# VectorE's queue order around a state's sums: where the product of k and b with R and the transpose of the inverse are issued

## The chip, the core and the metric

The kernel runs on one core of a Trainium2 chip. TensorE (PE) multiplies matrices into PSUM; VectorE (DVE), ScalarE (ACT) and GpSimd (POOL) work elementwise; SyncE (SP) issues most DMA transfers. Each engine takes the instructions of its own queue in order. The metric is the time of one execution on the device in microseconds; the median of several executions is compared.

## The reference

Three stages, all in float32. A recurrence over 768 steps for 32 pairs of batch and head, each with a state of 40 x 40; an MLP with squared ReLU over the 3072 tokens; and a layer of 8 experts that each token passes through by its largest logit.

```
for t in range(S):
    y[:, :, t] = einsum('bhd,bhde->bhe', rt, state)
    Sa = einsum('bhde,bhe->bhd', state, at)
    state = state * wt[:, :, None, :] - einsum('bhd,bhe->bhde', Sa, bt) + einsum('bhd,bhe->bhde', vt, kt)
...
h = x @ w_in; r = maximum(h, 0); x = (r * r) @ w_out
...
out[i] = gate_w[i] * (maximum(disp[e] @ w1[e], 0) @ w2[e])[pos[i]]
```

## The kernel before

The recurrence is turned into products of matrices. The 768 steps are cut into NS = 12 segments of 64 steps, each of NC = 2 chunks of 32. Within a chunk the steps depend on each other through a triangular system of 32 x 32 per head, so each segment needs the inverses of such matrices; the state goes from chunk to chunk. All segments run in a Python loop that is unrolled, over s and in it over c.

For a segment s these pieces matter:

- `scale(s)` (L133 to L160) loads w and then k and b (L138, L140), forms running products R of the decays w by a scan (L115), and multiplies k and b by them in place, two instructions (L146). A second scan (L128) gives their inverses, which scale a. It is a generator: its pieces are put between other work, for segment s + 2 during segment s, and the two instructions of L146 are traced after the first two slots of chunk (s, 1). The scan of L128 uses the one buffer that R has, so it follows L146.
- `lower(s, c)` (L162) multiplies a by k and b on PE and forms the triangular matrices; `invert(s)` (L183) transposes them on DVE (L187, tile `solve_al`) and then inverts them on GpSimd by 31 steps of two instructions each (recorded at L280, tiles `tmp` and `solve_tl`). `inverted(s)` (L203) transposes the result on DVE (L207, tile `solve_tf`), and ACT (L210) and DVE (L211) pick from it what is needed (tile `tt`).
- Chunk (s, c) goes through slots a to g (L1399 to L1450): `out` of the chunk before (PE product `py`, DVE L379 makes y), `right` (`pr`, reads the state zv and a), `solve` (`psa`, reads `tt`), `turn`, `inner`, `mix` (`ppq`, DVE L369 makes `lr`), `other` of the chunk before and `step`. The last two call `update` (L285): 16 products on PE per half of the heads into `pn`, and then two sums on DVE (L296) that write the next state, zk for `other` and zv for `step`. At a segment's end `other` also scales zk by a decay (L389).
- `fetch` (L248) loads the inputs of the next chunk and multiplies zk by `rx`, on DVE (L273) or on GpSimd.

In chunk (s, 0) `lower` and `invert` for segment s + 1 are traced, at the end of chunk (s, 1) `inverted(s + 1)`, behind both calls of `step`. Into the slots, pieces of the MLP of earlier tokens are put (`bursts`, L668): products `pl` on PE (L434), ReLU on ACT (L632), square on DVE (L634, tile `g`), a split into a high part on ACT (`gh`, L396) and a difference on DVE (`gl`, L397), and products that accumulate (`acc`, L616).

The order on each engine: PE's instructions keep the order of the program (`keep_in_program_order`), and GpSimd's of the recurrence are chained one behind another (`pool`, L277, with `issue_after`). For DVE, ACT and the DMA queues a scheduler orders the instructions ahead of time: it simulates the engines and issues, of what is ready in its simulation, what was traced first (or was given a higher priority). The hardware then follows this order. An instruction whose input comes later on the chip than in the simulation holds up its queue.

`tc.issue_after(i)` adds an edge from instruction i to each instruction of i's engine that is traced in its block: issue order alone, without a semaphore.

Of the kernel before, what the change touches and what calls it, by code (L numbers as in the profile page):

```python
# [16 lines left out]
ALU = mybir.AluOpType  # L17
# [13 lines left out]
C = 32  # L31
NC = SC // C
SEG = SC + 1
# [4 lines left out]
ROWS = 64 + D  # L38
# [19 lines left out]
BY_COL = [slice((1 - j) * 64, (1 - j) * 64 + D) for j in range(2)]  # L58
# [3 lines left out]
class Rwkv:  # L62
# [6 lines left out]
    def __init__(self, ctx, tc, ps, consts, keep, wd, kb, ad, rv, wl, tok, rng):  # L69
        self.tc, self.nc, self.ps = tc, tc.nc, ps  # L70
        self.c = consts
        self.src = dict(wd=wd, kb=kb, ad=ad, rv=rv, wl=wl, tok=tok)
        nc = self.nc
        p1 = ctx.enter_context(tc.tile_pool(name="rw1", bufs=1))
        self.p = ctx.enter_context(tc.tile_pool(name="rwr", bufs=1))
        self.dram = ctx.enter_context(tc.tile_pool(name="rwdram", bufs=2, space=DRAM))
        self.sq = p1.tile([128, 16, SEG], F32, name="seed_q")
        self.w = keep.tile([128, 1 + 16 * SEG], F32, tag="w_d", name="w_d")
        self.kb = keep.tile([128, 2, 16, SC], F32, tag="kb_d", name="kb_d")
        self.gb = p1.tile([128, 16, D], F32, name="g_b")  # L80


        self.a = [p1.tile([128, NC, 2, 16, C], F32, name=f"a{i}") for i in range(2)]
        self.zv = [p1.tile([128, 2, 16, D], F32, name=f"zv{i}") for i in range(2)]
        self.lr = [p1.tile([128, 2, 16, C], F32, name=f"lr{i}") for i in range(2)]
        self.zk = [p1.tile([128, 2, 16, D], F32, name=f"zk{i}") for i in range(2)]
        self.rng = rng

        nc.gpsimd.memset(self.w[32:64], 0.0)
        nc.vector.memset(self.kb[32:64], 0.0)  # L90
        nc.gpsimd.memset(self.a[0][32:64, :, 1], 0.0)
        nc.vector.memset(self.sq, 0.0)
        for t in (self.a[1][32:64, :, 1], *(t[32:64, 1] for t in self.zv + self.lr + self.zk), self.gb[32:64]):
            nc.gpsimd.memset(t, 0.0)
        for t in (self.zv[0], self.zk[0]):
            nc.gpsimd.memset(t[0:64, 1], 0.0)
            nc.gpsimd.memset(t[64:128, 0], 0.0)
        self.last = None
        self.pre, self.rt = {}, {}

    def psum(self, name):
# [31 lines left out]
    def scale(self, s):  # L133

        nc, src = self.nc, self.src
        w, kb, a = self.w, self.kb, self.a[s % 2]
        for j in range(2):
            nc.sync.dma_start(out=w[BY_COL[j]], in_=src["wd"][s, j])  # L138
        for j in range(2):
            nc.sync.dma_start(out=kb[BY_COL[j]], in_=src["kb"][s, j])  # L140

        pr = self.products(w, 16, ROWS, s)
        r = next(pr)
        yield
        for k in range(2):
            nc.vector.tensor_mul(kb[:ROWS, k], kb[:ROWS, k], r[:ROWS, :, 1:SEG])  # L146
            yield
        g = self.tile([128, 16], f"g64.{s}", 2)
        nc.vector.tensor_copy(g[:ROWS], r[:ROWS, :, 0])
        self.pre[s] = [g, [None] * NC, None]  # L150
        for j in range(2):
            nc.sync.dma_start(out=a[BY_COL[j], :, j].rearrange("p c n t -> p c (n t)"), in_=src["ad"][s, j])
        q = next(pr)
        yield
        for j in range(2):
            v = a[BY_COL[j], :, j]
            self.times(s == 0 and j == 0, out=v, in0=v, in1=q[BY_COL[j], :, 0:SC].rearrange("p n (c t) -> p c n t", c=NC))
        self.wl = self.tile([128, 1 + 10 * SEG], f"wl.{s}", 1)
        nc.sync.dma_start(out=self.wl, in_=src["wl"][s])
        yield  # L160
# [42 lines left out]
    def inverted(self, s):  # L203

        nc, tl = self.nc, self.tl
        tf = self.tile([128, C, 2, NC, H], f"solve.tf{s}", 2)
        nc.vector.transpose(out=tf.rearrange("p t u c h -> p (t u c h)"),  # L207
                            in_=tl[:, :, :, None].to_broadcast([128, C, C // 2, 2]))
        tt = self.tile([128, C, NC, H], f"tt.{s}", 2)
        nc.scalar.mul(tt, tf[:, :, 0], self.c["odd"][:, 0:1])  # L210
        i = nc.vector.scalar_tensor_tensor(out=tt, in0=tf[:, :, 1], scalar=self.c["odd"][:, 1:2], in1=tt,  # L211
                                           op0=ALU.mult, op1=ALU.add)
        self.pre[s][2] = tt
        return i.ins
# [33 lines left out]
    def fetch(self, s, c):  # L248
# [17 lines left out]
        for j in range(2):  # L266
            v = zk[BY_STEP[j], j].rearrange("p (h y) e -> p y h e", y=2)
            self.times(c == 1, out=v, in0=v, in1=rx[BY_STEP[j]])

    def times(self, fast, **k):  # L270

        if fast:
            self.nc.vector.tensor_tensor(op=ALU.mult, **k)  # L273
        else:
            self.pool(self.nc.gpsimd.tensor_tensor, op=ALU.mult, **k)
# [9 lines left out]
    def update(self, s, c, z, l, r, half):  # L285

        nc = self.nc
        pn = self.psum(f"pn{s}_{c}_{half}")[:, 0:8 * D].rearrange("p (n e) -> p n e", n=8)
        for n in range(8):
            i = half * 8 + n  # L290
            for j in range(2):
                rows = BY_STEP[j]
                self.mm(pn[BY_COL[j], n], lhsT=l[rows, j, i], rhs=r[rows, j, i], start=True, stop=True)
        for j in range(2):
            rows, ns = BY_COL[j], slice(half * 8, half * 8 + 8)
            nc.vector.tensor_tensor(out=z[c ^ 1][rows, j, ns], in0=z[c][rows, j, ns], in1=pn[rows], op=ALU.add)  # L296

    def right(self, s, c):

# [26 lines left out]

    def step(self, s, c, half):

        self.update(s, c, self.zv, self.zk[c], self.zv[c], half)

    def decay(self, s):

# [49 lines left out]

    def other(self, s, c, half):

        self.update(s, c, self.zk, self.zv[c], self.zk[c], half)
        if half == 1 and c == NC - 1 and s + 1 < NS:
            for j in range(2):
                v = self.zk[c ^ 1][BY_COL[j], j]
                self.nc.vector.tensor_mul(v, v, self.gb[BY_COL[j]])  # L389

# [1197 lines left out]
```

## Time and profile before

| | |
|---|---|
| median of 3 runs | 1195.83 us (1195.64 to 1196.54) |
| profiled execution | 1200.53 us, its span 1198.7 us |
| mean granted clock of PE | 0.927 of full |
| PE, DVE busy | 969.2 us (81%), 915.0 us (76%) |
| ACT, POOL busy | 491.7 us (41%), 570.5 us (48%) |
| segments of the recurrence in their steady state | about 187 to 821 us |
| experts | from about 880 us |

The busy shares are means over stages with different limits, so they don't tell what bounds a stage; the rows below are from the recurrence. A line such as L280 or L397 can be a helper's: L280 is all of GpSimd's recurrence, and L397 all differences of a split. PEld is the loading of weights into PE. "Idle before" is the time that an engine stood still ahead of an instruction, with what ended it. In the timelines neighbouring instructions of one kind are merged (x2, x4).

### The profile page before, as it was taken

What the parts mean: (1) busy time and instruction counts of PE and PEld (TensorE: products, weight loads), DVE (VectorE), ACT (ScalarE), POOL (GpSimd) and SP (SyncE); (2) the same over time, 40 slices, a digit from 0 to 9 for tenths busy, and PEclk for the clock granted to TensorE, in tenths of its full rate; (3) what the DMA queues carried; (4) which work ended last, traced back from release to release, by engine and by line L of the source; (5) the groups of instructions that cost most, each with busy time, mean ns of one, the idle gap of its engine ahead of it and who ended that gap; (6) DMA issues with size and microseconds to landing.
All of it is one profiled execution on the core that took longest, in us unless ns stands there. A gap on an engine that the chain in (4) does not pass through costs nothing.

```text
span 1198.7 us, 42394 instructions
## 1 busy us (share of the span) xinstructions
PE 969.2 (81%) x17749; PEld 901.3 (75%) x17749; DVE 915.0 (76%) x1925; ACT 491.7 (41%) x1301; POOL 570.5 (48%) x912
## 2 busy tenths in 40 slices
PE   1665446688989898979899797998989998999993
PEld 1554346677878787878788787887979998999993
DVE  8999887586878878686868788675867886777770
ACT  2443222233424232423324232342337475767760
POOL 5773936548283856648282847554000032222220
PEclk9999978898888888989989898999999999999997
DMA  8724524653343534343433535233267275767630
GB/s 243 201 80 132 153 57 108 232 141 116 102 122 102 132 104 125 107 132 107 131 116 86 132 104 141 87 118 92 86 193 245 77 238 183 218 198 223 219 95 8
DMA packets 87610, 164.37 MB, mean 137 GB/s; under 512 B 16313, under 2 KB 46651, under 8 KB 86444
## 3 DMA queue, kind: packets, MB, share of 16 engines
q1 hardware_dynamic: 78476, 141.47, 40.8%
q10 hardware_dynamic: 6048, 11.06, 3.2%
q0 software_dynamic: 2880, 8.98, 2.2%
q8 instruction: 143, 2.34, 0.8%
q14 instruction: 63, 0.52, 0.1%
HBM read 137.23 MB, written 16.29 MB: 128 GB/s over the span
## 4 chain that ended last, share of the span: by engine, by line
PE 29%; POOL 25%; DVE 20%; DMA 11%; issue 9%; ACT 4%; SPq 1%; POOLq 0%; ACTq 0%; DVEq 0%
POOL solve_tl L280 13%; POOL tmp L280 12%; PE upl L434 6%; PE uacc L1114 6%; PE acc L616 6%; PE pl L434 4%; DMA out_dram<-uo,room 2%; DVE zv L296 2%; DMA xg<-x_dram,room 2%; DVE gl L397 2%; DMA kb_d<-in_kb_dram 2%; DMA stage_hi<-in_w_out_dram 2%; DVE g L634 2%; DVE rq_r L115 1%; DVE solve_tf L207 1%
## 5 line engine op out<-in xcount | busy, mean ns | idle before, releaser
L280 POOL TENSOR_TENSOR solve_tl<-solve_tl,tmp 128x126 f32<-128x126 f32 (+22 forms) x372 | 195.0, 524 | 29.1
L280 POOL TENSOR_TENSOR tmp<-solve_al,solve_tl 128x126 f32<-128x126 f32 (+22 forms) x372 | 186.4, 501 | 33.1 <-DVE a L180 4.9
L616 PE MATMUL acc<-woh,gh 128*128 128x328 f32 x384 | 133.6, 348 | 12.9 <-ACT gh L396 12.7
L616 PE MATMUL acc<-woh,gl 128*128 128x328 f32 x384 | 130.1, 339 | 9.1 <-DVE gl L397 8.8
L616 PE MATMUL acc<-wol,gh 128*128 128x328 f32 x384 | 126.5, 329 | 0.0
L434 PE MATMUL pl<-x_hi,wi_hi 128*128 128x256 f32 x384 | 121.8, 317 | 1.7 <-ACT x_hi L446 1.7
L434 PE MATMUL pl<-x_lo,wi_hi 128*128 128x256 f32 x384 | 113.4, 295 | 11.0 <-DVE x_lo L449 11.0
L434 PE MATMUL pl<-x_hi,wi_lo 128*128 128x256 f32 x384 | 113.0, 294 | 0.0
L280 POOL MEMSET solve_tl<- 128x512 f32 x12 | 6.3, 527 | 215.4 <-DVE solve_al L187 215.4
L396 ACT CAST gh<-g 128x512 fp32r<-128x512 f32 x96 | 59.5, 620 | 120.2 <-DVE g L634 112.8
L1192 POOL DMA_INDIRECT out_dram<-uo,room x30 | 34.1, 1136 | 155.2 <-DVE uo L1181 84.1
L1122 POOL DMA_INDIRECT xg<-x_dram,room x30 | 30.4, 1012 | 141.6 <-DVE gl L397 61.4
L632 ACT ACTIVATE g<-pl 128x512 f32<-128x512 f32 x96 | 57.6, 600 | 97.2 <-PE pl L434 96.8
L397 DVE TENSOR_TENSOR gl<-g,gh 128x512 fp32r<-128x512 f32 x96 | 71.9, 749 | 26.4 <-ACT gh L396 26.3
L616 PEld LDWEIGHTS acc<-woh,gh 128*128 128x128 f32 x384 | 77.9, 203 | 17.0 <-ACT gh L396 13.3
L616 PEld LDWEIGHTS acc<-woh,gl 128*128 128x128 f32 x384 | 78.0, 203 | 15.3 <-DVE gl L397 14.6
L1114 PE MATMUL uacc<-w2h,hh 128*128 128x320 f32 x240 | 77.0, 321 | 12.0 <-ACT wi_hi L1070 12.0
L434 PEld LDWEIGHTS pl<-x_lo,wi_hi 128*128 128x128 f32 x384 | 78.1, 203 | 11.3 <-DVE x_lo L449 11.3
L283 PE MATMUL pr<-zv,a 104*32 104x40 f32 (+1 forms) x1536 | 44.0, 245 | 50.2 <-DVE zv L296 32.1
L434 PEld LDWEIGHTS pl<-x_hi,wi_hi 128*128 128x128 f32 x384 | 77.6, 202 | 6.5 <-ACT x_hi L446 2.1
L283 PEld LDWEIGHTS pr<-zv,a 104*32 104x32 f32 (+1 forms) x1536 | 31.7, 143 | 62.2 <-DVE zv L296 42.5
L616 PEld LDWEIGHTS acc<-wol,gh 128*128 128x128 f32 x384 | 78.2, 204 | 0.0
(272 smaller groups left out, 3030.6 us busy)
## 6 DMA issues: line engine op xcount, KB each, us to landing
wol<-wol SPq DMA_DIRECT2D x96, 328.0 KB
w<-in_w_dram SPq DMA_DIRECT2D x30, 640.0 KB
w<-in_w_dram SPq DMA_DIRECT2D x30, 512.0 KB
kb_d<-in_kb_dram SPq DMA_DIRECT2D x24, 320.0 KB
zv<-in_tok_dram SPq DMA_DIRECT2D x48, 160.0 KB
zk<-in_tok_dram SPq DMA_DIRECT2D x48, 160.0 KB
rx<-rt SPq DMA_DIRECT2D x192, 40.0 KB
w<-in_w_dram SPq DMA_DIRECT2D x30, 256.0 KB
```

Of the source, the lines that this page charges most:

```text
L280: self.last = f(*a, **k).ins
L283: self.tc.keep_in_program_order(self.nc.tensor.matmul(*a, **k))
L296: nc.vector.tensor_tensor(out=z[c ^ 1][rows, j, ns], in0=z[c][rows, j, ns], in1=pn[rows], op=ALU.add)
L396: return (nc.scalar.copy(hi, x).ins, nc.vector.tensor_tensor(out=lo, in0=x, in1=hi.bitcast(F32), op=ALU.subtract).ins)
L397: nc.vector.tensor_tensor(out=lo, in0=x, in1=hi.bitcast(F32), op=ALU.subtract).ins)
L434: tc.keep_in_program_order(tc.nc.tensor.matmul(out, lhsT=a, rhs=b, start=n == 0, stop=n == len(seq) - 1))
L616: self.tc.keep_in_program_order(self.nc.tensor.matmul(*a, **k))
L632: nc.scalar.activation(g, pl, AF.Relu)
L634: nc.vector.tensor_tensor(out=g, in0=pl, in1=g, op=ALU.mult)
L1114: self.tc.keep_in_program_order(self.nc.tensor.matmul(*a, **k))
L1122: nc.gpsimd.indirect_dma_start(out=xg[:, 0:DX], out_offset=None, in_=self.x1, in_offset=bass.IndirectOffsetOnAxis(ap=self.idx[2 * j + t], ...
L1192: self.nc.gpsimd.indirect_dma_start(out=self.out, out_offset=bass.IndirectOffsetOnAxis(ap=self.to[:, n:n + 1], axis=0), in_=o[:, t], in_of ...
```

## The change

`step` and `other` now remember the last of their instructions on DVE, in `sums[0]` (last sum of zv) and `sums[1]` (last sum of zk, or its scaling by the decay). A new function `behind(n)` opens `issue_after` for the first n of them. The two products of k and b with R (L146) are traced behind both, the transpose of the inverse (L207) behind the last sum of zv. Nothing else changes: no instruction is added, removed or altered. For segments 0 and 1 of `scale` and segment 0 of `inverted` no sums have been traced yet, so they have no edges; that leaves ten pairs of products and eleven transposes with one.

```diff
--- before.py
+++ after.py
@@ -96,6 +96,7 @@
             nc.gpsimd.memset(t[0:64, 1], 0.0)
             nc.gpsimd.memset(t[64:128, 0], 0.0)
         self.last = None
+        self.sums = []
         self.pre, self.rt = {}, {}
 
     def psum(self, name):
@@ -143,7 +144,8 @@
         r = next(pr)
         yield
         for k in range(2):
-            nc.vector.tensor_mul(kb[:ROWS, k], kb[:ROWS, k], r[:ROWS, :, 1:SEG])
+            with self.behind(2):
+                nc.vector.tensor_mul(kb[:ROWS, k], kb[:ROWS, k], r[:ROWS, :, 1:SEG])
             yield
         g = self.tile([128, 16], f"g64.{s}", 2)
         nc.vector.tensor_copy(g[:ROWS], r[:ROWS, :, 0])
@@ -204,8 +206,9 @@
 
         nc, tl = self.nc, self.tl
         tf = self.tile([128, C, 2, NC, H], f"solve.tf{s}", 2)
-        nc.vector.transpose(out=tf.rearrange("p t u c h -> p (t u c h)"),
-                            in_=tl[:, :, :, None].to_broadcast([128, C, C // 2, 2]))
+        with self.behind(1):
+            nc.vector.transpose(out=tf.rearrange("p t u c h -> p (t u c h)"),
+                                in_=tl[:, :, :, None].to_broadcast([128, C, C // 2, 2]))
         tt = self.tile([128, C, NC, H], f"tt.{s}", 2)
         nc.scalar.mul(tt, tf[:, :, 0], self.c["odd"][:, 0:1])
         i = nc.vector.scalar_tensor_tensor(out=tt, in0=tf[:, :, 1], scalar=self.c["odd"][:, 1:2], in1=tt,
@@ -267,6 +270,13 @@
             v = zk[BY_STEP[j], j].rearrange("p (h y) e -> p y h e", y=2)
             self.times(c == 1, out=v, in0=v, in1=rx[BY_STEP[j]])
 
+    def behind(self, n):
+
+        order = ExitStack()
+        for i in self.sums[:n]:
+            order.enter_context(self.tc.issue_after(i))
+        return order
+
     def times(self, fast, **k):
 
         if fast:
@@ -293,7 +303,8 @@
                 self.mm(pn[BY_COL[j], n], lhsT=l[rows, j, i], rhs=r[rows, j, i], start=True, stop=True)
         for j in range(2):
             rows, ns = BY_COL[j], slice(half * 8, half * 8 + 8)
-            nc.vector.tensor_tensor(out=z[c ^ 1][rows, j, ns], in0=z[c][rows, j, ns], in1=pn[rows], op=ALU.add)
+            i = nc.vector.tensor_tensor(out=z[c ^ 1][rows, j, ns], in0=z[c][rows, j, ns], in1=pn[rows], op=ALU.add)
+        return i.ins
 
     def right(self, s, c):
 
@@ -326,7 +337,7 @@
 
     def step(self, s, c, half):
 
-        self.update(s, c, self.zv, self.zk[c], self.zv[c], half)
+        self.sums[:1] = [self.update(s, c, self.zv, self.zk[c], self.zv[c], half)]
 
     def decay(self, s):
 
@@ -382,11 +393,12 @@
 
     def other(self, s, c, half):
 
-        self.update(s, c, self.zk, self.zv[c], self.zk[c], half)
+        last = self.update(s, c, self.zk, self.zv[c], self.zk[c], half)
         if half == 1 and c == NC - 1 and s + 1 < NS:
             for j in range(2):
                 v = self.zk[c ^ 1][BY_COL[j], j]
-                self.nc.vector.tensor_mul(v, v, self.gb[BY_COL[j]])
+                last = self.nc.vector.tensor_mul(v, v, self.gb[BY_COL[j]]).ins
+        self.sums[1:] = [last]
```

## Rows read from the trace of the kernel before

**Rows 1.** The page's part 1: busy time of each engine, share of the span, instructions.

```profile
PE 969.2 (81%) x17749; PEld 901.3 (75%) x17749; DVE 915.0 (76%) x1925; ACT 491.7 (41%) x1301; POOL 570.5 (48%) x912
```

**Rows 2.** Windows, a segment each: length, busy PE PEld DVE ACT POOL, clock, DMA.

```profile
390.50:456.70 66.20, 58.24 (x1325) 52.86 (x1324) 52.18 (x88) 22.82 (x52) 40.67 (x69) 0.90 0.42 117
sum 601.50, PE 512.30 PEld 465.85 DVE 464.88 ACT 203.88 POOL 363.70; mean PE 56.92 PEld 51.76 DVE 51.65 ACT 22.65 POOL 40.41
```

**Rows 3.** Chain of waits, 394 to 466 us, shares by line.

```profile
by line: POOL solve_tl L280 23.9%; POOL tmp L280 18.2%; DMA kb_d<-in_kb_dram 10.5%; PE acc L616 10.0%; PE pl L434 8.8%; issue 5.6%; DVE kb_d L146 3.7%; PE pa L283 2.9%; DVE zv L296 2.7%; PE pn L283 2.3%; DVE gl L397 2.2%; PE ppq L283 2.0%; 
```

**Rows 4.** Timeline of GpSimd: start, length, what; in brackets idle before and its releaser.

```profile
456.84 0.53 POOL L280 MEMSET solve_tl<- 128x512 f32 x1 [20.50 <-DVE solve_al L187]
```

**Rows 5.** Windows: from a transpose of the inverse (L207) to the next L187.

```profile
428.01:455.45 27.44, 24.88 (x628) 22.23 (x628) 25.13 (x45) 13.18 (x31) 8.18 (x4) 0.88 0.30 92
```

**Rows 6.** Waits, 187 to 821 us, DVE and PE: total us, times, longest.

```profile
DVE solve_tf L207 <- POOL solve_tl L280: 49.3, 10, 9.9
DVE kb_d L146 <- DMA kb_d<-in_kb_dram: 21.9, 9, 2.9
...
PE py L283 <- DVE zk L389: 44.8, 18, 8.7
```

**Rows 7.** Timeline of DVE at the products of k and b.

```profile
397.17 2.56 DVE L146 TENSOR_TENSOR kb_d<-kb_d,rq_r 104x1024 f32<-104x1024 f32 x2 [2.32 <-DMA kb_d<-in_kb_dram]
399.76 1.78 DVE L389 TENSOR_TENSOR zk<-zk,g_b 40x640 f32<-40x640 f32 x2
...
402.30 1.00 DVE L296 TENSOR_TENSOR zv<-zv,pn 40x320 f32<-40x320 f32 x2
...
404.19 1.00 DVE L296 TENSOR_TENSOR zv<-zv,pn 40x320 f32<-40x320 f32 x2
```

**Rows 8.** Timeline of PE: py, the products for the sums of zv, psa.

```profile
400.76 0.23 PE L283 MATMUL py<-zk,lr 104*32 104x40 f32 x2 [3.26 <-DVE zk L389]
...
424.27 1.42 PE L283 MATMUL pn<-zv,zk 64*40 64x40 f32 x64
...
438.27 1.29 PE L283 MATMUL psa<-rh,tt 32*32 32x40 f32 x64
```

**Rows 9.** Timeline of DVE at the transpose of the inverse.

```profile
428.01 1.25 DVE L207 STREAM_TRANSPOSE solve_tf<-solve_tl 128x1024 f32<-128x1024 f32 x1 [4.14 <-POOL solve_tl L280]
429.18 0.65 DVE L634 TENSOR_TENSOR g<-pl,g 128x512 f32<-128x512 f32 x1
429.86 1.00 DVE L296 TENSOR_TENSOR zv<-zv,pn 40x320 f32<-40x320 f32 x2
430.79 0.88 DVE L211 SCALAR_TENSOR_TENSOR tt<-solve_tf,ct,tt 128x512 f32<-128x512 f32 x1
431.70 1.00 DVE L296 TENSOR_TENSOR zv<-zv,pn 40x320 f32<-40x320 f32 x2
432.62 1.65 DVE L397 TENSOR_TENSOR gl<-g,gh 128x512 fp32r<-128x512 f32 x1
```

**Rows 10.** Timeline of DVE, the second transpose of the inverse.

```profile
154.19 1.25 DVE L207 STREAM_TRANSPOSE solve_tf<-solve_tl 128x1024 f32<-128x1024 f32 x1 [8.22 <-POOL solve_tl L280]
```

**Rows 11.** Timeline: a difference on DVE, and three steps of the inverse on GpSimd.

```profile
394.17 0.68 DVE L397 TENSOR_TENSOR gl<-g,gh 128x512 fp32r<-128x512 f32 x1
...
393.25 0.31 POOL L280 TENSOR_TENSOR solve_tl<-solve_tl,tmp 128x58 f32<-128x58 f32 x1
...
394.00 1.02 POOL L280 TENSOR_TENSOR solve_tl<-solve_tl,tmp 128x56 f32<-128x56 f32 x1
...
403.10 0.38 POOL L280 TENSOR_TENSOR tmp<-solve_al,solve_tl 128x110 f32<-128x110 f32 x1
```

**Rows 12.** Windows: PE ahead of the solve.

```profile
434.33:441.00 6.67, 6.67 (x116) 6.15 (x117) 6.24 (x13) 2.70 (x9) 2.01 (x1) 0.61 0.29 89
```

**Rows 13.** Timeline of DVE and of PE in the segment at 224 us.

```profile
224.24 1.25 DVE L207 STREAM_TRANSPOSE solve_tf<-solve_tl 128x1024 f32<-128x1024 f32 x1 [9.88 <-POOL solve_tl L280]
...
234.20 0.31 PE L283 MATMUL pr<-zv,a 104*32 104x40 f32 x2 [4.07 <-DMA zv<-in_tok_dram]
```

## The prediction

> **What bounds the kernel now.** I read the page first: over the span TensorE (PE) is busy 81%, VectorE (DVE) 76% and GpSimd (POOL) 48% [rows 1]. No engine is full, so the question is which wait ends last where the change acts. That is the recurrence, from about 187 to 821 us: nine segments that repeat every 66.8 us (601.5 / 9), in which PE works 56.9 us and DVE 51.7 us in the mean [rows 2]. Next I read the chain of waits over one segment: GpSimd's two lines of the inverse hold 24% and 18% of it, the longest part; most of the rest is PE work [rows 3]. The reader should see a loop in it. GpSimd inverts for segment s+1; DVE transposes the result (L207); from that the solve of (s+1, 0) starts on PE; after it PE, ACT and DVE come to the transposed input (L187) of the next inverse, and GpSimd starts again. GpSimd itself stood idle 20.5 us before that start [rows 4]. So the period is the time of one inverse and its start plus the stretch from L207 to L187. In the segment shown that stretch is 27.44 us (428.01 to 455.45) [rows 4, 5], and the inverse about 66.2 - 27.4 - 1.2 = 37.5 us.
>
> Then I read who makes DVE wait between 187 and 821 us: the transpose waits for GpSimd in ten segments, 49.3 us together, and the product of k and b waits for its load in nine, 21.9 us [rows 6]. DVE runs its queue in order, so what stands behind these two waits too. The timeline shows what that is. Behind the products of k and b (idle 2.32 us, then 2.56 us of work) stand the scaling of zk and the state's sums at 402.30 and 404.19 [rows 7]; PE, which needs them, idles (3.26 us before py in this place alone [rows 8], 44.8 us over the nine segments for the scaled zk [rows 6]). Behind the transpose, which waited 4.14 us, stand one square of the MLP, the four sums of zv and a difference gl [rows 9], though the products for those sums had ended at 425.69 (424.27 + 1.42) [rows 8].
>
> **The change part by part.** It adds no instruction and takes none away; it adds issue order on one engine, without semaphores. The edges concern ten pairs of products and eleven transposes. In one transpose (154.19) [rows 10] the sums had been issued long before, so ten are left; of the products nine pairs stand ahead of sums now, as [rows 7] shows for one.
>
> *The transpose.* Each of the ten goes behind the last sum of its segment. The wait for GpSimd is not removed: the inverse ends when it ends. What changes is that DVE does useful work in the wait. The four sums (2 x 1.00), the square (0.65) and gl leave the stretch after the transpose. The square and gl carry no edge, but they are traced before the transpose and become ready about with the sums, so I expect the planner to let them pass too; that is a choice, and its failure is a rival. gl took 1.65 us where it stood [rows 9], while GpSimd multiplied beside it, and about 0.68 at 394.17 in an empty surrounding [rows 11]. So 3.33 to 4.30 us leave the stretch; I take 4.30, since that is what these instructions cost there. DVE was busy 25.13 us of the 27.44 us [rows 5], so the stretch is nearly DVE's own length and the removal carries through; of the 2.31 us in which it idled I count half, 1.15 us, as going too, since PE, which DVE waited for in them, comes earlier. The bounds of that are 0 and 2.31.
>
> Against it stands what is added beside the inverse. A step of GpSimd that should last about 0.3 us lasted 1.02 when gl ran beside it; beside the sums, which read PSUM, a step lasted 0.38 [rows 11]. So gl costs the inverse 0.7 us, and the sums nothing. (The Trainium skill, SBUF — State Buffer, Who interferes with whom, says why only gl counts: an instruction of VectorE with two inputs in SBUF blocks a GpSimd instruction that reads SBUF, one with at most one does not. The rows agree; if every sum blocked as well, the gain of a segment would shrink by 2.0 us.)
>
> Per segment: 4.30 + 1.15 - 0.7 = 4.75 us; bounds 3.33 - 0.7 = 2.6 and 4.30 + 2.31 = 6.6.
>
> PE must be able to follow. The inverse's second half was ready when L211 ended (430.79 + 0.88 = 431.67) [rows 9], but the solve's product psa began at 438.27 [rows 8], 6.6 us later, because PE was still waiting for sums and gl and then ran its accumulation at a granted clock of 0.61 [rows 12], mostly the lower level of 1.2 GHz, after idling. With the sums early, that work is done before the transpose. So PE gives up to 6.6 us, and DVE is the tighter of the two.
>
> *The products of k and b.* They move behind the scaling of zk and four sums. Their load, which ended at about 397.2, is then there before they are reached: DVE saves the 2.32 us of idling, and the sums come 2.32 + 2.56 = 4.9 us earlier. For whom? The queue behind the products (the scan of L128, L115) comes no later than now, since what passes it is no more than what stood behind it. PE's idle time of 3.26 us and the slow clock after it go. But all this happens beside the running inverse, which has more than 20 us to go, so on the loop it is worth 0: PE and DVE arrive earlier at the wait for the inverse. I count it at nothing, and what it does is provide cover: it lets the sums end before GpSimd does (without it they would end at about 427.7, and with square and gl at 429, about 1 us behind it). Its bounds are 0 and all of the idling that PE has, the rival below. No DMA is issued by a moved instruction; the queue of SP keeps its order as far as the trace can tell.
>
> *The sum.* Nine stretches from transpose to L187 at 4.75 us: 42.8 us. The first of them had a longer stall (9.88 us), but behind it PE then waited for a load of zv until 234.20 [rows 13], so I give it no more than the others. The tenth transpose has no inverse behind it and PE is nearly full from there on; I count it at nothing. The profiled execution took 1200.53 us (span 1198.7); it would take 1157.8. The median of the runs is 4.70 us lower, 1195.83; carried over, **1153.1 us**. Own range with the bounds: 9 x 2.6 = 23 to 9 x 6.6 = 59 us, 1136 to 1173.
>
> **The rivals.**
> 1. *PE becomes the bound.* If DVE is relieved further (the products' part counts after all, other DVE work also moves ahead of the transpose), the period falls until PE is full. PE works 56.9 us of 66.8 [rows 2]; with 1.4 us of unavoidable idling the gain is 9 x 8.5 = 76 us: 1120 (1110 to 1136). For it: most of PE's idling is at the two places that the change touches. Against: the stretch holds 25 us of DVE work that is not moved. (The Trainium skill, Trainium Kernel Development and Optimization, Performance Expectations, holds matmul busy time to be a poor measure and weight-load busy a good one; that is 51.8 us here in [rows 2], and the floor would be 135 us lower than now. The matmuls of the MLP follow each other without a gap in the stretches where PE works, so I keep 56.9.)
> 2. *Another wait takes the place.* The planner leaves square and gl, or y, behind the transpose; then PE stands as before, and only the sums' 2.0 us leave: 9 x 2.0 = 18 us, 1178 (1173 to 1191).
> 3. *It does nothing*, as with the transpose at 154.19: 1195.8. Against: in the other ten the order visibly changes.
> 4. *Slower: the transpose comes late.* It is now held behind sums that may end after the inverse. What decides is whether they end more than 4.30 us behind it, since that much has left the stretch. Today they would end about even with it. The mechanism would be the products (2.56 us) and the scan behind them, newly ahead of the MLP's differences, holding up PE and so pn by some 6 us: 2.2 us lost in nine segments, 1216. Against: these waits of PE are now spent at the same place anyway.
>
> **How the numbers follow.** Chances: forecast 0.53, PE the bound 0.13, another wait 0.17, nothing 0.05, slower 0.12. The range leaves out rival 4, rival 3 and a quarter of rival 1: 1115 to 1191, about 0.80. A measurement of this kernel can tell about 0.2%, 2.4 us, from no change; faster by more than that 0.83, within 0.05, slower 0.12.
>
> **What would show it.** In the profile after, the sums of zv must stand ahead of L207 in ten segments and of L146 in nine; the wait of L146 for its load should be gone, that of L207 for GpSimd smaller but not gone (1 to 4 us each); the period about 62 us; L207 to L187 about 22 to 24 us; the inverse 37 to 39 us. If the stretch from L207 to L187 stays at 27 us, the step "DVE's moved work leaves the stretch" is wrong. If the inverse grows by over 2 us, GpSimd's price is. If the transpose starts well after GpSimd has ended, rival 4 is at work.

## The result, and the profile after

The changed kernel takes 1179.62 us (median of four runs, 1177.35 to 1186.99) against 1195.74 (four runs, 1193.28 to 1196.54): a ratio of 0.9865, 95% interval 0.9828 to 0.9901. It is faster by 16.1 us, where the forecast was 42.7, and the time lies 6.6 us above the upper of the forecast's own bounds (1173). The profiled execution took 1179.72 us, 20.8 less than the profiled one of before.

Of part 1 of the page VectorE's line moved most against [rows 1]: the same 1925 instructions, which no edit altered, take 934.5 us where they took 915.0.

```profile
PE 958.6 (81%) x17749; PEld 897.2 (76%) x17749; DVE 934.5 (79%) x1925; ACT 490.7 (42%) x1301; POOL 585.2 (50%) x912
```

The waits of VectorE and TensorE between 187 and 821 us, which answer to [rows 6]:

```profile
DVE solve_tf L210 <- POOL solve_tl L290: 37.6, 10, 8.2
...
DVE zk L283 <- DMA zk<-in_tok_dram: 20.0, 8, 3.1
PE py L293 <- issue: 0.5, 1, 0.5
```

The order came out as meant. The transpose's wait for GpSimd fell from 49.3 to 37.6 us, the products' wait for their load and TensorE's 44.8 us for the scaled zk are gone. The second line is new: VectorE now comes so early to the product of zk with `rx` that it waits there for the load of zk.

VectorE at the transpose of the inverse, which answers to [rows 9]:

```profile
415.62 0.99 DVE L306 TENSOR_TENSOR zk<-zk,pn 40x320 f32<-40x320 f32 x2
...
417.24 1.00 DVE L306 TENSOR_TENSOR zv<-zv,pn 40x320 f32<-40x320 f32 x2
418.17 0.68 DVE L409 TENSOR_TENSOR gl<-g,gh 128x512 fp32r<-128x512 f32 x1
418.88 1.00 DVE L306 TENSOR_TENSOR zv<-zv,pn 40x320 f32<-40x320 f32 x2
422.13 1.25 DVE L210 STREAM_TRANSPOSE solve_tf<-solve_tl 128x1024 f32<-128x1024 f32 x1 [2.25 <-POOL solve_tl L290]
423.30 0.65 DVE L646 TENSOR_TENSOR g<-pl,g 128x512 f32<-128x512 f32 x1
423.88 0.47 DVE L390 TENSOR_TENSOR y<-py,qt 128x320 f32<-128x320 f32 x1
424.28 1.51 DVE L214 SCALAR_TENSOR_TENSOR tt<-solve_tf,ct,tt 128x512 f32<-128x512 f32 x1
425.82 5.42 DVE L348 TENSOR_TENSOR zv<-zv,g 40x640 f32<-40x640 f32 x2
```

The four sums and gl stand ahead of the transpose, which waits 2.25 us where it waited 4.14. But the scaling of zv by the decay (L348) takes 5.42 us for two instructions. GpSimd at that time:

```profile
422.06 3.18 POOL L290 TENSOR_TENSOR zk<-zk,rx 64x640 f32<-64x640 f32 x2
425.20 5.37 POOL L290 TENSOR_TENSOR a<-a,rq_q 40x1024 f32<-40x1024 f32 x2
449.30 0.53 POOL L290 MEMSET solve_tl<- 128x512 f32 x1 [18.73 <-DVE solve_al L189]
```

In the kernel before, the same scaling came after GpSimd's products of a, and took 1.67 us. What stood beside them there was work that reads PSUM (two sums, a square and y), gl (1.65 us [rows 9]) and the clamp of L124. The two engines in the kernel before:

```profile
431.08 5.26 POOL L280 TENSOR_TENSOR a<-a,rq_q 40x1024 f32<-40x1024 f32 x2
...
435.19 1.51 DVE L124 TENSOR_SCALAR rq_r<-rq_r 128x650 f32<-128x650 f32 x1
436.73 1.67 DVE L337 TENSOR_TENSOR zv<-zv,g 40x640 f32<-40x640 f32 x2
```

Taken singly, GpSimd's two products of a in the changed kernel end at 427.83 and 430.57, and VectorE's two scalings at 428.51 and 431.24. So each scaling, 0.82 us long elsewhere, ended 0.7 us after the product beside it had ended: its length followed the end of that product.

The stretches from the inverse's transpose to the next L187 (now L189), as windows: length, busy PE, PEld, DVE, ACT and POOL with their counts, clock, DMA. First the kernel before, its first stretch and the sum of all nine:

```profile
224.24:257.09 32.85, 24.31 (x634) 22.23 (x635) 28.66 (x49) 13.40 (x31) 8.53 (x4) 0.84 0.52 163
...
sum 254.59, PE 222.99 PEld 200.96 DVE 227.22 ACT 118.97 POOL 74.33; mean PE 24.78 PEld 22.33 DVE 25.25 ACT 13.22 POOL 8.26
```

Then the changed kernel, its first, the one that answers to [rows 5], and the sum:

```profile
227.85:252.32 24.47, 19.46 (x489) 18.24 (x490) 21.76 (x38) 11.59 (x27) 9.87 (x4) 0.79 0.48 146
...
422.13:447.92 25.79, 22.76 (x507) 20.52 (x508) 24.55 (x40) 11.84 (x29) 8.28 (x4) 0.87 0.29 87
...
sum 229.19, PE 193.01 PEld 175.17 DVE 215.54 ACT 106.00 POOL 76.29; mean PE 21.45 PEld 19.46 DVE 23.95 ACT 11.78 POOL 8.48
```

That gives the account of the two profiled executions. The nine stretches are 25.4 us shorter: 8.4 in the first alone, 17.0 in the other eight, 2.1 each. The ten inverses from L187 to the transpose are together 9.3 us longer (379.2 to 388.5 us, 0.93 each). The first of them starts 2.0 us later, and what follows the last transpose, with the experts, is 6.7 us shorter. Sum: -25.4 + 9.3 + 2.0 - 6.7 = -20.8 us.

In a stretch of 25.79 us VectorE is busy 24.55, so it idles 1.24 where it idled 2.31, but its work shrank only from 25.13 to 24.55 us, though 4.30 us had been moved out. Three instructions account for 3.35 of the 3.7 us that came back: the scaling (+3.75), the selection tt (0.88 to 1.51; it now starts 1.0 us before GpSimd's product of zk ends, where it started 0.3 us before) and the clamp, which now comes after GpSimd has ended and takes 0.48 instead of 1.51 (-1.03).

ScalarE ahead of the solve, and the solve on TensorE (this last line answers to the last of [rows 8]):

```profile
425.27 0.84 ACT L123 ACTIVATE over<-rq_r,ct 128x650 f32<-128x650 f32 x1 [1.14 <-POOL zk L290]
...
426.76 0.83 ACT L123 ACTIVATE over<-rq_r,ct 128x650 f32<-128x650 f32 x1
427.50 0.19 ACT L123 ACTIVATION_READ_ACCUMULATOR over<-rq_r,ct 128x1 f32 x1
427.59 0.40 ACT L318 COPY rh<-pr 128x320 f32<-128x320 f32 x1
...
428.05 1.29 PE L293 MATMUL psa<-rh,tt 32*32 32x40 f32 x64 [0.67 <-ACT rh L318]
```

psa begins 5.92 us after the transpose, where it began 10.26 after it. It still waits for ScalarE's copy of the right-hand side, behind two range tests of the decays that ScalarE queued ahead, and these wait for GpSimd's product of zk. So there were two candidates for what ends the stretch now: VectorE's queue with its collisions, and TensorE's chain from psa to the last product of a (pa, read by the mask am on VectorE). The same trace already speaks against the end of that chain:

```profile
442.49 1.10 PE L293 MATMUL pa<-kb_d,a 40*32 40x64 f32 x64
...
447.58 0.42 DVE L178 TENSOR_TENSOR am<-pa,ct 128x256 f32<-128x256 f32 x1
```

The last product had ended for 4.0 us when VectorE came to it, so what ends last is VectorE's queue; TensorE can still lengthen it where VectorE waits earlier in the stretch.

### The profile page after: what moved, and what is told of

Read it like the earlier page. It is cut to its first block, busy times and chain, and to the rows that moved or that the text cites. A ratio compares the mean times of both kernels' runs of the same rounds, so it can differ in the third digit from the quotient of the medians.

```text
span 1177.9 us, 42361 instructions
## 1 busy us (share of the span) xinstructions
PE 958.6 (81%) x17749; PEld 897.2 (76%) x17749; DVE 934.5 (79%) x1925; ACT 490.7 (42%) x1301; POOL 585.2 (50%) x912
## 4 chain that ended last, share of the span: by engine, by line
PE 32%; POOL 23%; DVE 17%; DMA 10%; issue 9%; ACT 4%; SPq 2%; POOLq 0%; DVEq 0%; ACTq 0%
POOL solve_tl L290 10%; POOL tmp L290 10%; PE upl L446 7%; PE pl L446 7%; PE uacc L1126 6%; PE acc L628 5%; DMA zk<-in_tok_dram 3%; DMA out_dram<-uo,room 2%; POOL zk L290 2%; PE pn L293 2%; DVE rq_r L116 2%; DVE rq_q L129 1%; DMA xg<-x_dram,room 1%; SPq L268 1%; DVE g L646 1%
## 5 line engine op out<-in xcount | busy, mean ns | idle before, releaser
L290 POOL TENSOR_TENSOR solve_tl<-solve_tl,tmp 128x126 f32<-128x126 f32 (+22 forms) x372 | 201.3, 541 | 29.1
L628 PE MATMUL acc<-woh,gl 128*128 128x328 f32 x384 | 124.9, 325 | 8.2 <-DVE gl L409 7.8
L446 PE MATMUL pl<-x_hi,wi_hi 128*128 128x256 f32 x384 | 127.6, 332 | 0.7 <-ACT x_hi L458 0.7
L446 PE MATMUL pl<-x_lo,wi_hi 128*128 128x256 f32 x384 | 118.5, 309 | 9.9 <-DVE x_lo L461 9.9
L446 PE MATMUL pl<-x_hi,wi_lo 128*128 128x256 f32 x384 | 117.9, 307 | 0.0
L446 PEld LDWEIGHTS pl<-x_lo,wi_hi 128*128 128x128 f32 x384 | 83.5, 218 | 10.1 <-DVE x_lo L461 10.1
L646 DVE TENSOR_TENSOR g<-pl,g 128x512 f32<-128x512 f32 x96 | 65.5, 683 | 27.3 <-ACT g L644 26.4
L446 PEld LDWEIGHTS pl<-x_hi,wi_hi 128*128 128x128 f32 x384 | 82.6, 215 | 5.7 <-ACT x_hi L458 1.1
L628 PEld LDWEIGHTS acc<-woh,gl 128*128 128x128 f32 x384 | 75.5, 197 | 11.9 <-DVE gl L409 11.9
L446 PEld LDWEIGHTS pl<-x_hi,wi_lo 128*128 128x128 f32 x384 | 83.1, 216 | 0.0
L293 PE MATMUL pr<-zv,a 104*32 104x40 f32 (+1 forms) x1536 | 33.9, 229 | 57.3 <-DVE zv L306 27.4
```

Of the source, the lines that this page charges most:

```text
L290: self.last = f(*a, **k).ins
L293: self.tc.keep_in_program_order(self.nc.tensor.matmul(*a, **k))
L446: tc.keep_in_program_order(tc.nc.tensor.matmul(out, lhsT=a, rhs=b, start=n == 0, stop=n == len(seq) - 1))
L628: self.tc.keep_in_program_order(self.nc.tensor.matmul(*a, **k))
L646: nc.vector.tensor_tensor(out=g, in0=pl, in1=g, op=ALU.mult)
```

## The experiments

They ran on three chips; the kernel before took 1201.46 us (runs 1 to 4), 1197.27 (5 to 8) and 1200.08 (9 to 12) there, and ratios are to these. "Stretch" and "inverse" are as above; stretch sums are of nine, inverse sums of ten.

**1 and 2. Each edge alone.** In tf_only the products of k and b are traced without their edges, in kb_only the transpose:

```diff
-            with self.behind(2):
+            with self.behind(0):      # tf_only
-        with self.behind(1):
+        with self.behind(0):          # kb_only
```

> Only the transpose of the inverse is queued behind the sums; the products of k and b are left to the scheduler. Theory A (the loop is one inverse plus the stretch from the transpose to the next transposed input, and what the products' edge wins lies beside the inverse and is worth nothing): most of the gain stays, 1175 to 1185 us, the stretch about 25 to 26 us in the steady segments, the wait of the products for their load back at about 2.3 us each. Rival B (the products' edge is needed as cover, since the sums otherwise end behind the inverse): the transpose starts well after GpSimd has ended and less than half of the gain is left, 1188 to 1194 us.

> Only the products of k and b are queued behind the sums. Theory A: nothing of it is on the loop, 1192 to 1197 us, the stretch from the transpose to the next transposed input stays at 27 to 28 us, while the wait of the products for their load is gone and zk's product waits for its load in its place. Rival B (PE's progress counts by itself): 1180 to 1188 us.

Measured: tf_only 1189.41 us, ratio 0.9898 (0.987 to 0.9925); kb_only 1189.34, 0.9889 (0.9855 to 0.9923). By the ratio tf_only came out as its theory A had it, and kb_only as its rival B had it, though for the most part in one stretch. Stretches of tf_only: 33.7, then 25.8 to 26.0 and 24.0; of kb_only: 24.5, then 26.4 to 27.6. The inverses' sums are 386.6 and 382.6 us. So the 2.1 us of each later stretch belong to the transpose's edge, and the 8.4 us of the first to the products' edge alone. By itself that edge also takes 0.8 us from each later stretch; together with the other it adds nothing there. I had given it 0.

**3. The collision taken away by order.** The scaling of zv is queued behind the last sum of zk's first half, past GpSimd's products (for that the sums are also traced ahead of it):

```diff
+                with self.tc.issue_after(self.sums[1]) if n == D else ExitStack():
-                self.nc.vector.tensor_mul(v, v, g[BY_COL[j], :, None].to_broadcast([D, 16, n]))
+                    self.nc.vector.tensor_mul(v, v, g[BY_COL[j], :, None].to_broadcast([D, 16, n]))
```

> As the changed kernel, but the scaling of zv by the decay on VectorE is queued behind the sums of the other state's first half, so that it no longer runs beside GpSimd's products of a. Theory A (the gain was given back there: 5.4 us for the two scalings where 1.7 us were enough): the scalings take 1.6 to 1.8 us again, the stretch falls from 25.8 to about 22 us, the time by some 8 x 3.7 = 30 us to about 1150 us. Rival C (PE's late solve sets the stretch, VectorE has slack in it): the scalings get shorter, the stretch and the time stay, 1177 to 1182 us.

Measured: 1178.05 us, 0.9828 (0.9791 to 0.9865); stretch 25.4. The scaling is short again, as expected, but the place beside GpSimd is taken by the next in the queue:

```profile
424.51 1.65 DVE L410 TENSOR_TENSOR gl<-g,gh 128x512 fp32r<-128x512 f32 x1 [0.95 <-ACT gh L409]
426.08 2.48 DVE L125 TENSOR_SCALAR rq_r<-rq_r 128x650 f32<-128x650 f32 x1
...
431.54 1.65 DVE L349 TENSOR_TENSOR zv<-zv,g 40x640 f32<-40x640 f32 x2
```

The clamp takes 2.48 us and gl 1.65, where they took 0.48 and 0.68. VectorE's work fell from 24.6 to 23.6 us, the stretch by 0.4, and the time can't be told from the changed kernel's. Removing one victim doesn't remove the collision.

**4. The collision taken away at its source.** GpSimd's products of a are left out from segment 2 on, so that part of the result isn't computed:

```diff
+            if s < 2:
-            self.times(s == 0 and j == 0, out=v, ...)
+                self.times(s == 0 and j == 0, out=v, ...)
```

> As the changed kernel, but GpSimd's products of a with the inverse running products are left out from segment 2 on, so what it computes is not the reference. Theory A: without them the scalings of zv take 1.6 to 1.8 us beside an idle GpSimd, the pick of the inverse about 0.9 us instead of 1.5 us, and the stretch falls to 21 to 22.5 us, the time to 1145 to 1152 us. Rival C: the stretch stays above 25 us, the time at 1177 to 1182 us.

Measured: 1172.73 us, 0.9771 (0.975 to 0.9791). The windows of one stretch and the sum:

```profile
478.50:503.17 24.67, 21.07 (x504) 19.14 (x503) 20.77 (x39) 11.93 (x29) 3.04 (x2) 0.93 0.32 92
...
sum 223.15, PE 188.15 PEld 171.68 DVE 184.02 ACT 106.87 POOL 27.88; mean PE 20.91 PEld 19.08 DVE 20.45 ACT 11.87 POOL 3.10
```

VectorE's work falls by 3.8 us to 20.77, so that much of its 24.55 was collision with these products. But the stretch falls only to 24.67 (24.8 in the mean of nine), so neither theory's time came out, and psa still begins 5.9 us after the transpose. VectorE's work alone isn't the bound any more once it is relieved. What holds it up now:

```profile
489.69 0.60 ACT L645 ACTIVATE g<-pl 128x512 f32<-128x512 f32 x1 [2.26 <-PE pl L447]
...
490.32 0.69 DVE L647 TENSOR_TENSOR g<-pl,g 128x512 f32<-128x512 f32 x1 [1.81 <-ACT g L645]
```

VectorE's square waits for ScalarE's ReLU, and that for the products pl of the MLP, which follow the late psa on TensorE. From 285 to 730 us these waits of VectorE sum to 28.1 us, in the changed kernel to 11.9. So TensorE's chain acts in the middle of the stretch; the last product of a again ends early, 3.5 us before VectorE comes to it.

**5. TensorE relieved alone.** ScalarE's range tests are queued behind its copy of the right-hand side:

```diff
-        self.nc.scalar.copy(self.rh, pr)
+        self.rh_copy = self.nc.scalar.copy(self.rh, pr).ins
...
+                with self.tc.issue_after(self.rh_copy) if s > 0 else ExitStack():
```

> As the changed kernel, but ScalarE's two range tests (which wait for GpSimd's products of zk) are queued behind the copy of the right-hand side, so that they no longer hold up that copy and the copy of y. Theory D (after the change PE's late solve, held up in ScalarE's queue, and the low clock after that idling set the stretch): the solve starts 3.5 to 4.5 us after the transpose instead of 5.9 us, the stretch falls from 25.8 to 23.5 to 24.5 us, ratio to the kernel before 0.975 to 0.981. Rival E (the scan on VectorE ahead of the next transposed input ends last, whatever PE does): the solve is earlier, the stretch stays above 25 us, ratio 0.984 to 0.989.

Measured: 1180.29 us, 0.984 (0.9796 to 0.9884). psa begins 3.78 us after the transpose and TensorE's last product of a ends 19.2 after it, 2 us earlier than before the edit, yet the stretch is 26.2 us. VectorE shows why: gl now comes in time to stand beside GpSimd, ahead of the scaling, and the two together take 6.24 us where they took 6.10.

```profile
424.51 2.68 DVE L410 TENSOR_TENSOR gl<-g,gh 128x512 fp32r<-128x512 f32 x1
427.23 3.56 DVE L349 TENSOR_TENSOR zv<-zv,g 40x640 f32<-40x640 f32 x2
```

VectorE's work stays at 24.59 us. So in the changed kernel VectorE's queue sets the stretch.

**9. Both relieved.** Edits 4 and 5 together; the same part of the result isn't computed.

> The changed kernel without GpSimd's products of a with the running products of the decays (the two of each segment from the third on; that part of the computation is left out) and with ScalarE's range tests queued behind its copy of the solve's right-hand side. Alone, the first left VectorE with 20.8 us of work in a stretch of 24.7 us between the two transposes, and the second brought TensorE's last product of a 2 us forward but not the end of the stretch. Theory: two chains of nearly one length, VectorE's queue and TensorE's products, end the stretch together, so taking a little from both must bring more than the sum of the single effects: psa about 3.8 us after the inverse's transpose, stretch 21.5 to 23 us, about 16 us faster than without the products of a alone would be if nothing were added (ratio to the kernel before 0.965 to 0.970). Rival: a third thing bounds the stretch (GpSimd, a load, or TensorE's clock after idling); then the stretch stays above 24 us and the ratio at 0.975 to 0.980.

Measured: 1157.28 us, 0.9652 (0.9612 to 0.9692).

```profile
474.63:496.96 22.33, 20.40 (x499) 18.57 (x497) 20.73 (x40) 12.29 (x29) 3.03 (x2) 0.92 0.35 101
...
sum 206.73, PE 177.17 PEld 161.73 DVE 183.70 ACT 108.58 POOL 27.71; mean PE 19.69 PEld 17.97 DVE 20.41 ACT 12.06 POOL 3.08
```

The sums of the stretches: 229.2 in the changed kernel, 223.2 without the products (-6.0), 231.0 with the range tests later (+1.8), 206.7 with both (-22.5). Two things of nearly one length set the stretch, VectorE's own work and its waits for what TensorE does behind psa, and only relief of both brings it in. That sum comes near the one that I had forecast for the change alone (254.6 - 49.1 = 205.5 us), and so does the ratio; but this kernel has a further edge and leaves work out, so the nearness doesn't bear the forecast out.

**6. More work moved out of the stretch.** The scan of w and its clamp are queued behind the next transpose L189, that is beside the inverse:

```diff
+        with self.tc.issue_after(self.al) if s > 1 else ExitStack():
-        r = next(pr)
+            r = next(pr)
```

> As the changed kernel, but the scan of the decays of a later segment (2.3 us, and its clamp, 0.7 us) is queued on VectorE behind the next transposed input, for which nothing waits there. Rival E: the stretch falls by 2.5 to 3 us to about 23 us, ratio to the kernel before 0.966 to 0.974. Theory D alone (PE sets the stretch): 0.3 to 1 us, since PE's last product for the inverse then ends last, ratio 0.979 to 0.985.

Measured: 1189.54 us, 0.9937 (0.9911 to 0.9963), 9.3 us above over_later on the same chip. The later stretches fall to 23.8 to 24.5 us, nearly as expected, but each later inverse grows from about 39.4 to 42.0: 2.33 us of scan and 0.70 us of clamp cost GpSimd 2.5 us. What leaves the stretches (229.2 to 214.6 us in sum) is more than given back by the inverses (388.5 to 411.6).

**7 and 8. Edits 3, 5 and 6 together** (over_scan_decay), and with the load of k and b behind that of zk in SyncE's queue (four).

> As the changed kernel with three edges more: the range tests behind the copy of the right-hand side, the scan behind the next transposed input, the scaling of zv behind the other state's sums. If theories D and E each hold a part: stretch 20 to 22 us, ratio 0.950 to 0.965. If PE's work between solve and the second lower product is the floor (13 us, and 3 to 4 us on either side): 21 to 23 us, ratio 0.960 to 0.970.

> As the kernel with three further edges, and the load of k and b is queued on SyncE behind the load of zk. Theory A (what lies beside the inverse is worth nothing): the wait of zk's product for its load, 2.2 to 3.1 us in each segment, goes, and the time stays within 0.4% of the kernel with three further edges. Rival (that wait counts): 8 x 2.5 = 20 us less, 1.7%.

Measured: 1183.65 us, 0.9868 (0.9818 to 0.9919), and 1181.3, 0.9841 (0.9788 to 0.9894). Both have later stretches of 23.3 us and inverses of 42.0, longer than either theory of run 7 had the stretch. The wait of VectorE for zk's load, 8.8 us in the first of the two, is gone in the second without a difference that can be told, and the period from transpose to transpose is 65.2 and 65.1 us: beside the inverse that wait costs nothing here. That the new wait of 20.0 us that the change made costs nothing either is likely from this, but wasn't tried.

**10. The first stretch.** In the kernel before, the clearing of the output moves one chunk later:

```diff
-                if s == 1 and c == 0:
+                if s == 1 and c == 1:
```

> The kernel before, with the clearing of the output buffer and of its neighbour (the sixteen transfers that SyncE issues from 213 to 224 us) put one chunk later; nothing else is changed. Theory: in the kernel before the first steady stretch (32.85 us against 27 to 29 in the others) is long because the load of the state's v stands behind these transfers in SyncE's queue, and the changed kernel wins 8.4 us there only because its planner issues that load in the middle of them. Then the stretch falls to 26 to 28.5 us and the rest stays: 5 to 7 us, ratio 0.994 to 0.996. Rival: the stall lies at the products of k and b, not at the transfers; then the first stretch stays above 31 us and the time as it was, ratio 0.998 to 1.002.

It rests on SyncE's queue (SPq), first in the kernel before, then in the changed one:

```profile
212.99 10.97 SPq L1306 DMA_DIRECT2D out_dram<-zero  x16
...
229.25 1.84 SPq L254 DMA_DIRECT2D zv<-in_tok_dram  x2
```

```profile
208.21 3.17 SPq L1318 DMA_DIRECT2D out_dram<-zero  x5
...
212.40 4.08 SPq L1318 DMA_DIRECT2D out_dram<-zero  x6
216.58 2.45 SPq L257 DMA_DIRECT2D zv<-in_tok_dram  x2
...
220.36 2.71 SPq L1318 DMA_DIRECT2D out_dram<-zero  x5
```

Measured: 1196.96 us, 0.9976 (0.9948 to 1.0004): no difference that can be told. The first stretch does fall, from 32.85 to 28.9 us, but the inverse behind it grows from 38.5 to 42.2, since the two scans that had run inside the stretch (at 250.27 and 252.32 us in the kernel before) now run beside it, at 274.17 and 277.52. TensorE's wait for the load (4.07 us [rows 13]) is gone, but with the scans 6.5 us of VectorE's work left the stretch too (28.66 to 22.20 us), so the run doesn't show which of the two shortened it. That the time follows was wrong. In the changed kernel both scans still end before L189 (243.61 and 246.75, L189 at 252.32), and there the 8.4 us stay won. That they go with the place of the load in SyncE's queue the runs with one edge show as well: tf_only issues it at 233.62, behind all transfers, and its first stretch is 33.7 us; kb_only issues it at 215.08, among them, and has 24.5.

**11 and 12. The products of a moved to VectorE, beside the changed kernel.** a_on_vector gives GpSimd's products of a to VectorE and has edits 3 and 5; after_again is the changed kernel on the same chip.

```diff
-            self.times(s == 0 and j == 0, out=v, ...)
+            self.times(s != 0 or j == 0, out=v, ...)
```

> The changed kernel with GpSimd's products of a moved to VectorE, with ScalarE's range tests behind its copy of the solve's right-hand side and with the decay's scaling of the state zv behind the last sum of zk. The work added to VectorE (two products a segment) has two inputs in SBUF. Theory: what collided with GpSimd behind the inverse (5.42 us for scalings that take 1.67 us alone) goes, since GpSimd has nothing there any more; the stretch between the transposes falls from 25.8 to 22 to 23.5 us even with the added products; if the added products run inside the stretch the inverse stays at 39 to 40 us and the kernel comes to a ratio of 0.972 to 0.980 to the kernel before. Rival: the added products lie beside the inverse or lengthen the stretch themselves, and what is won goes back (inverse 41 us or more, or stretch 25 us): ratio 0.984 to 0.990, no better than the changed kernel.

> The changed kernel itself, on the chip of the other three, so that they are compared with it there: ratio to the kernel before 0.983 to 0.990, as measured.

Measured: 1171.23 us, 0.9774 (0.9698 to 0.9849; single runs 1162.43 to 1177.6), and 1183.8 us, 0.9848 (0.9797 to 0.9899; 1176.61 to 1186.86). The median is 12.6 us lower, though the runs touch at 1177 us and the intervals overlap, so it isn't shown to be the faster of the two. Where the products went, and the stretches:

```profile
407.98 2.66 DVE L284 TENSOR_TENSOR a<-a,rq_q 40x1024 f32<-40x1024 f32 x2
...
sum 203.82, PE 177.66 PEld 161.79 DVE 185.07 ACT 107.50 POOL 27.17; mean PE 19.74 PEld 17.98 DVE 20.56 ACT 11.94 POOL 3.02
```

What took GpSimd 5.37 us takes VectorE 2.66. The stretches sum to 203.8 us against 230.2 in after_again, but the products lie beside the inverse, as the rival had it, and the inverses' sum is 402.7 against 388.9. Of 26.4 us 13.8 are given back. The ratio falls in the theory's range, not in the rival's, which its interval just reaches.

## Why the prediction was right in sign and wrong in size

**What held.** The order: sums, gl and one square passed the transpose, as I chose to expect, and the products' wait is gone. The idle time of VectorE in a stretch fell by 1.07 us (forecast 1.15). The inverse grew by 0.93 us (forecast 0.7). Rival 4 didn't come about: the last sum had ended 2.25 us before the transpose could start (422.13). TensorE had time to give (psa 4.3 us earlier, of "up to 6.6"), and VectorE was the tighter of the two (run 5), though by little (run 4). Of the signs named, the period is 65.3 us instead of about 62 and the stretch 25.8 instead of 22 to 24. (Of the sums one is off without weight: 66.2 - 27.4 - 1.2 is 37.6, not 37.5.)

**What failed: "the removal carries through".** This is the step of 4.30 us. The work did leave the stretch, and 3.7 of the 4.30 us came back, 3.35 of them in three instructions that changed their length. I had read [rows 5] as if VectorE's 25.13 us were work of a fixed length. They depend on what stands beside GpSimd's products of zk and a, which follow the inverse at once. Before, the sums stood there, which read PSUM and took 1.00 us beside GpSimd's products [rows 9], as those of zk took 0.98 beside an idle GpSimd (at 440.92 in the kernel before); I moved out mostly what isn't held up, and what moved up into the place is. The rows had the warning: gl took 1.65 us there and 0.68 elsewhere [rows 9, 11]. I used that to size the gain of moving gl, and not to ask what would take gl's place. (The Trainium skill, SBUF — State Buffer, Who interferes with whom, names the reverse direction as well: two SBUF inputs on VectorE contend with a GpSimd instruction that reads SBUF, a tensor_scalar can too, and which was issued first decides who blocks. The traces agree: the scaling 0.82 to 2.70 us each, the clamp 0.48 to 2.48, while GpSimd's two products of a took 5.2 to 5.4 us in the eight later stretches of both kernels. I had weighed the rule only for GpSimd's steps.)

The step behind it, "DVE is the tighter of the two", hid a second bound. Run 4 shows it: without the collisions with the products of a the nine stretches sum to 223.2 us, still 17.7 above the forecast's 205.5. psa comes 5.9 us after the transpose there too, behind ScalarE's range tests and so behind GpSimd's product of zk, and VectorE then waits for what follows on TensorE. I had priced what TensorE could give, not what it waits for. Of the 23.7 us by which the stretches miss their sum, 6.0 go with these collisions alone and 22.5 with the range tests as well (run 9).

Eight stretches at 2.1 and one at 8.4 us make 25.4 instead of 9 x 5.45 = 49.1: 23.7 us of the miss. The inverse's ten times 0.93 instead of nine times 0.7 add 3.0 us, the later start of the first inverse 2.0, and the tail gives 6.7 back: 22.0, the 21.9 by which the profiled time of 1179.72 us missed my 1157.8. The remaining 4.6 us are the carry-over to the median: the profiled run of before lay 4.70 us above its median, that of after 0.10.

**The products of k and b, "worth 0 on the loop".** Right for eight stretches once the transpose's edge is there (25.8 us with or without), wrong for the first, where the whole 8.4 us go with them (runs 1 and 2). I saw the load of zv that PE waited for in that segment [rows 13], and wrote that SyncE's queue keeps its order. It didn't: with the new order on VectorE the planner put that load among the transfers of the clearing, 12.7 us earlier. How much of the 8.4 us is the load's, and how much is VectorE's work that then ended before the transpose (28.66 us fell to 21.76), stays open (run 10).

**The rivals.** Rival 2 gave 1178 us and comes within 2 us of the time, but that is luck: it had square and gl, or y, stay behind the transpose and TensorE stand as before. y did stay behind (423.88), but square and gl passed, and psa came 4.3 us earlier. Inside the stretch no new wait took the place; the same instructions got longer. The name of the cause that I lacked is a collision handed on in a queue. Rival 1, PE becoming the bound, needs VectorE relieved; run 4 shows that VectorE then waits for TensorE long before TensorE is full (20.9 us busy of 24.8).

**What stays open.** The tail behind the last transpose. It was 6.7 us shorter in the changed kernel's first profile, 1.3 in after_again (376.4 against 377.7 us). Over all profiles it is 367.3 to 376.4 us in the eleven with the transpose's edge and 377.7 to 378.7 in the three without, so some part of it may belong to the tenth transpose, which I gave 0. It wasn't tried by itself. Nor was what ends the 23.0 us of run 9, where VectorE idles 2.6 us and PE 3.3 in the mean.

## What to carry to other kernels

When work is moved out of a stretch, list what moves up into its place and what GpSimd does beside that place; price the newcomers by the slow row of their kind, not by the quiet one. In these traces work that reads PSUM is a good neighbour for GpSimd's products, work with two SBUF inputs is a bad one, and reordering alone hands the collision to the next in the queue. Where an engine's own work and its waits for another engine are nearly as long, relieve both before judging either.

## What was not expected of the hardware

- Beside GpSimd's products of a, two scalings of 40x640 elements on VectorE took 5.42 us instead of 1.67, and GpSimd 5.37 instead of 5.26: nearly the whole difference fell on VectorE. (GpSimd isn't free of it: the same pair took 4.64 us at 79 us in the kernel before and 6.45 in the changed kernel's first stretch.) Beside the inverse the price falls on GpSimd: 3.0 us of scan and clamp lengthened it by 2.5 us.
- A clamp with one tensor input (TENSOR_SCALAR, 128x650) is held up as well: 0.48, 1.51 or 2.48 us, by what GpSimd did beside it.
- The same two products of a take 5.37 us on GpSimd and 2.66 us on VectorE.
